# Pooled attention and grouped experts: keys and values in five blocks of 32 rows a pair, and another order for batches 0 to 2

## The chip, the cores and the metric

The kernel runs on one core of one Trainium2 chip. The metric is the device time of one execution in microseconds (us). PE (TensorE) does the matmuls, DVE (VectorE) and POOL (GpSimd) element-wise work, ACT (ScalarE) copies, casts and activations. SP (SyncE) issues most DMAs; ACT issues some. A DMA "lane" below is one of eight semaphores that the framework hands round: an issue waits until the DMA that last used its lane has landed.

## The reference

For 8 batches of 8 heads with 576 rows of 64, keys and values are averaged over groups of 8 rows (72 pooled rows a head), and attention runs over them. Its 4608 tokens of 512 numbers then go to a mixture of 16 experts (4 groups of 4), one expert a token.

```python
k_p = k.reshape(B, H, Sp, pool, D).mean(axis=3); v_p = ...      # pool = 8, Sp = 72
scores = scale * q @ k_p.T ; attn = softmax(scores)
x = (attn @ v_p).transpose(0, 2, 1, 3).reshape(B * S, H * D)
g_idx = argmax(x @ w_group) ; g_w = softmax(...)[g_idx]
e_idx = argmax(x @ w_expert[g]) ; e_w = softmax(...)[e_idx]
out[token] = g_w * e_w * (relu(x @ w1[g, e]) @ w2[g, e])        # 512 -> 1024 -> 512
```

## The kernel before

**Stages.** One batch at a time. A batch has a main expert, the one that most of its tokens choose; its tokens all go through that expert's weights, and the result is scaled by a gate that is zero for tokens of other experts. Those are done at the end, in a part called Left.

The order of the work is written out by hand, in four strings: START (batch 0's attention), FIRST (batch 0's experts beside batch 1's attention), STEADY (batches 1 to 6) and LAST. A piece such as `a.kr:0:f` is a method of a class with its arguments. The letter says whose: a is this batch's attention, m its experts, n the next batch's attention, w the next batch's weights, x the batch after that, t set-up work, l the part Left. PE, SP, DVE and POOL follow the strings in order; ACT does so in START and FIRST, and a scheduler of the framework orders it elsewhere.

**Attention (class Att).** The rows of two heads are a pair: 144 pooled rows of 512 numbers (8 rows of 64). `load_k` brings the first 128 of them for two pairs in one DMA of 128 partitions; `load_v` the same rows of v, as four blocks of 32 rows on the 32 partitions of each pair, in four DMAs; `load_r` the last 16 rows of k or v of each pair into a tile `rem`. `kr` sums the eight rows of k by three additions in place on DVE (`fold`: 256, 128, 64 wide), `vr` those of v on POOL, `rr` sums `rem` by a reduction on DVE, `vm` (POOL) splits the block that both heads share. `kb` (ACT) copies the sums into two masked halves, one for each head, `kt` transposes them on PE and copies the result to `kT`. `qt` (batch 0, by matmuls with the identity) or `qb` (DVE, other batches) transposes a chunk of 128 rows of q, `sc` makes its scores on PE, `mx`, `sb`, `su_`, `nm` are the softmax (DVE; the exponent on ACT; the last product on POOL), `pt` turns the result on DVE. `av` multiplies with the values on PE and casts the result to fp32r on ACT, `avd` gives the remainder on DVE: tokens `xt` as two parts. `rt`, `route`, `count`, `gates`, `keep_x` route the tokens. `guess_x` and `guess_e` guess the main expert ahead of time from the sums of v for batches 0 and 1; later batches count (`main_expert`). Either ends in a register that SP loads and that the weights' DMAs wait for.

**Experts (class Moe).** `load` brings a quarter of the first (1) or second (2) weights, 0.52 MB. `split` casts it to fp32r on ACT and takes the remainder on POOL. `up:f:h` is 12 matmuls for rows f of the first product and half h of the tokens (256 or 320), with an ACT evacuation; `upd` its remainder on DVE; `down:z` 8 matmuls of the second product.

`t.warm:n` are n matmuls of ones with nothing to compute. Tiles for k, `kv`, rotate over two buffers; v has one (`vv`).

Line 198 is `load_r`, 190 `load_v`, 184 `load_k`, 211 `load_q`, 251 to 253 `fold`, 246 `kb`, 266 `kt`, 283 `qt`, 431 `guess_x`, 438 `guess_e`, 494 `load`, 501 and 502 `split`, 516 `up`, 542 and 553 `down`, 348 `av`, 357 `avd`, 312 and 314 `sb`, 321 `su_`.

Of the kernel before, what the change touches and what calls it, by code (L numbers as in the profile page):

```python
# [8 lines left out]
F32 = mybir.dt.float32  # L9
F32R = mybir.dt.float32r  # L10
# [3 lines left out]
ALU = mybir.AluOpType  # L14
# [4 lines left out]
SP = 72  # L19
# [22 lines left out]
a.mx:4 a.sb:4 m.up:3:0 m.split:1:3:p m.load:2:1 m.load:2:2 m.load:2:3 n.load_qb:0 n.load_qb:1 n.load_qb:2 n.load_qb:3 m.upd:3:0 a.pt:3 a.su_:4 a.nm:4:p m.up:4:0 m.upd:4:0
m.up:5:0 m.upd:5:0 a.pt:4 m.up:6:0 m.upd:6:0 a.av:256:320 m.up:7:0 m.upd:7:0 a.avd:256:320 m.split:2:0:p
a.rt:0:256 m.up:0:1 m.upd:0:1 n.vr:0:p a.rt:256:320 m.up:1:1 m.upd:1:1 n.rr m.split:2:1:p n.vr:1:p n.vm m.up:2:1 m.upd:2:1 a.route n.kr:0:f
m.up:3:1 m.upd:3:1 n.guess_x m.split:2:2:p m.up:4:1 m.upd:4:1 a.count n.guess_e m.up:5:1 m.upd:5:1 n.kr:1:f n.kb a.gates m.split:2:3:p
# [9 lines left out]
m.load:2:3 m.up:1:1 m.upd:1:1 n.sc:2 n.mx:2 n.sb:2 n.qb:3 n.pt:1 x.load_r:k x.load_k:0 x.load_k:1 x.load_r:v x.load_v  # L55
# [5 lines left out]
m.down:0 n.rt:256:320 x.kr:0:f m.down:1 x.kr:1:f m.down:2 n.route m.down:3 m.down:4 n.main_expert w.load:1:0 w.load:1:1 w.load:1:2 w.load:1:3  # L61
x.rr x.kb m.down:5 x.qb:0 n.gates n.keep_x m.down:6 x.vr:0 x.vr:1 m.down:7 w.split:1:0 w.load:2:0 x.kt m.down:8 m.down:9
# [813 lines left out]
```

## Time and profile before

| what | value |
|---|---|
| median of 3 runs | 586.15 us (583.66 to 586.68) |
| profiled execution: time, span | 585.75 us, 584.0 us |
| busy: PE | 524.3 us (90%) |
| busy: DVE, POOL, ACT | 349.6, 242.6, 216.7 us |
| 0 to 40.4 us | START: up to the first matmul of `up` |
| 40.4 to 145.7 us | FIRST |
| 145.7 to 516.2 us | six times STEADY, 61.8 to 62.1 us each but the last (61.0) |
| 516.2 to 584.0 us | LAST and Left |

The profiled execution took 585.75 us, of which 584.0 are the span that the trace covers. Busy times are those of one engine and overlap with the others'.

### The profile page before, as it was taken

The page shows a single profiled execution, that of the slowest core. Times are in us where ns is not written, and L with a number is a line of the kernel's source. Part 1 is how long each engine was busy: PE and PEld are TensorE (multiplying, and loading weights), DVE is VectorE, ACT ScalarE, POOL GpSimd, SP SyncE. Part 2 cuts the span into 40 slices and gives each one's busy share as a digit, 9 for nine tenths or more (in the row PEclk, how much of TensorE's full clock was granted, in tenths as well). Part 3 has the DMA queues.
Part 4 walks back from the last instruction along what each step waited for, and adds up shares of the span by engine and source line. Part 5 has one row for each costly group of instructions (what it writes and reads, how often), then busy time and mean ns, then how long its engine had stood idle before and what let it go on. Part 6 is the DMA issues. An engine that isn't in the chain of part 4 may idle for free.

```text
span 584.0 us, 15213 instructions
## 1 busy us (share of the span) xinstructions
PE 524.3 (90%) x6125; PEld 460.0 (79%) x6125; DVE 349.6 (60%) x1031; ACT 216.7 (37%) x428; POOL 242.6 (42%) x201
## 2 busy tenths in 40 slices
PE   6777868696899999899989998999999998999995
PEld 6665757475797899789978897889878997899864
DVE  3367586559866567456955495738665673358702
ACT  1233431134443354334532554244433543244211
POOL 3254630353482347424660558053814572231300
PEclk9799988889999999999999999999999999999999
DMA  8196602870493639455762758095927210563731
GB/s 219 29 260 206 71 0 71 246 128 20 143 210 64 210 109 219 63 177 157 177 107 91 236 148 140 21 371 153 200 56 223 94 38 2 182 187 122 250 122 48
DMA packets 113521, 81.33 MB, mean 139 GB/s; under 512 B 70538, under 2 KB 89994, under 8 KB 113064
## 3 DMA queue, kind: packets, MB, share of 16 engines
q1 hardware_dynamic: 107872, 70.54, 47.0%
q10 hardware_dynamic: 5544, 9.74, 4.8%
q8 instruction: 50, 0.82, 0.6%
q14 instruction: 23, 0.19, 0.1%
q0 software_dynamic: 32, 0.04, 0.0%
HBM read 75.01 MB, written 28.38 MB: 177 GB/s over the span
## 4 chain that ended last, share of the span: by engine, by line
PE 70%; DVE 16%; DMA 6%; ACT 3%; issue 2%; SPq 1%; POOL 1%; ACTq 0%; DVEq 0%; POOLq 0%
PE mm L516 30%; PE mm L542 21%; PE sc L298 4%; PE mm L553 4%; PE sc L348 4%; PE tp L365 2%; DMA kv<-in_k_dram 2%; DMA out_dram<-y 2%; DVE xt L357 1%; DMA rem<-in_k_dram 1%; SPq L220 1%; DVE p L312 1%; ACT xt L353 1%; DMA rem<-in_v_dram 1%; DVE su L321 1%
## 5 line engine op out<-in xcount | busy, mean ns | idle before, releaser
L502 POOL TENSOR_TENSOR w<-sw,w 128x1024 fp32r<-128x1024 f32 x61 | 144.9, 2383 | 163.3 <-ACT w L501 163.3
L516 PE MATMUL mm<-xt,w 128*128 128x256 f32 (+1 forms) x1536 | 206.4, 292 | 4.0 <-POOL w L502 2.0
L516 PEld LDWEIGHTS mm<-xt,w 128*128 128x128 f32 x1536 | 196.0, 192 | 11.7 <-issue 3.4
L542 PE MATMUL mm<-w,ht 128*128 128x512 f32 x768 | 178.0, 385 | 0.0
L542 PEld LDWEIGHTS mm<-w,ht 128*128 128x128 f32 x768 | 142.8, 190 | 21.6 <-issue 1.9
L327 POOL TENSOR_TENSOR p<-p,su 128x576 f32<-128x576 f32 (+1 forms) x40 | 42.1, 1054 | 119.7 <-DVE su L322 88.1
L518 ACT ACTIVATE ht<-mm 128x256 fp32r<-128x256 f32 (+1 forms) x128 | 52.1, 410 | 96.3 <-PE mm L516 96.0
L501 ACT CAST w<-sw 128x1024 fp32r<-128x1024 f32 x64 | 65.9, 1043 | 25.2 <-DMA sw<-in_moe_w_dram 25.2
L528 DVE SCALAR_TENSOR_TENSOR ht<-mm,ht 128x160 fp32r<-128x160 f32 (+2 forms) x192 | 38.9, 258 | 30.4 <-ACT ht L518 29.6
L314 ACT ACTIVATE p<-p 128x576 f32<-128x576 f32 (+1 forms) x40 | 25.5, 637 | 75.6 <-DVE p L312 65.7
L308 DVE TENSOR_REDUCE mx<-sc 128x8 f32<-128x576 f32 (+1 forms) x40 | 27.6, 690 | 35.8 <-PE sc L298 35.8
L348 PE MATMUL sc<-pT,v 32*64 32x256 f32 (+1 forms) x384 | 29.8, 443 | 16.6 <-DVE xt L357 9.7
L298 PE MATMUL sc<-kT,qT 64*32 64x72 f32 x2304 | 32.5, 232 | 9.4 <-DVE qT L290 5.1
L298 PEld LDWEIGHTS sc<-kT,qT 64*32 64x32 f32 x2304 | 25.6, 106 | 17.6 <-issue 11.7
L524 DVE SCALAR_TENSOR_TENSOR ht<-mm,ht 128x256 fp32r<-128x256 f32 x64 | 26.0, 408 | 22.0 <-ACT ht L518 21.4
L547 ACT ACTIVATE y<-mm,gm 128x512 f32<-128x512 f32 x32 | 21.9, 684 | 42.9 <-PE mm L542 42.9
L348 PEld LDWEIGHTS sc<-pT,v 32*64 32x64 f32 x384 | 14.9, 142 | 23.1 <-issue 19.7
L320 DVE TENSOR_REDUCE su<-p 128x8 f32<-128x576 f32 (+1 forms) x40 | 27.1, 678 | 7.9 <-ACT p L314 7.7
L334 DVE STREAM_TRANSPOSE pT<-p 128x640 f32<-128x640 f32 (+1 forms) x40 | 30.3, 757 | 2.6 <-POOL p L327 2.6
L348 PE MATMUL tp<-pT,v 32*64 32x256 f32 (+1 forms) x384 | 31.5, 443 | 0.0
L553 PE MATMUL mm<-w,ht 128*128 128x512 f32 x128 | 29.5, 381 | 0.0
L312 DVE TENSOR_TENSOR p<-sc,mx 128x576 f32<-128x576 f32 (+1 forms) x40 | 27.9, 696 | 1.4
(196 smaller groups left out, 487.9 us busy)
## 6 DMA issues: line engine op xcount, KB each, us to landing
sw<-in_moe_w_dram SPq DMA_DIRECT2D x72, 512.0 KB
xscr<-xt SPq DMA_DIRECT2D x8, 2304.0 KB
vv<-in_v_dram SPq DMA_DIRECT2D x32, 256.0 KB
out_dram<-y ACTq DMA_DIRECT2D x32, 256.0 KB
q<-in_q_dram SPq DMA_DIRECT2D x112, 72.0 KB
kv<-in_k_dram SPq DMA_DIRECT2D x14, 512.0 KB
pT<-xscr SPq DMA_DIRECT2D x4, 1152.0 KB
kv<-in_moe_w_dram SPq DMA_DIRECT2D x4, 512.0 KB
```

The lines of the kernel that those rows point to most:

```text
L298: nc.tensor.matmul(ps[32 * g:32 * g + 32, x, SP * t:SP * t + SP], lhsT=s.qT[c][64 * x:64 * x + 64, g, 32 * t:32 * t + 32], rhs=s.kT[64 * x ...
L312: tt(out=p.rearrange("p t (x s) -> p x t s", x=2), in0=s.ss[c][:, :, 0:SP * w].rearrange("p x (t s) -> p x t s", s=SP), in1=bc(s.m[c][:, : ...
L327: (nc.vector if eng == "v" else nc.gpsimd).tensor_tensor(out=p, in0=p, in1=bc(s.su[c][:, 0:w], SP), op=ALU.mult)
L334: nc.vector.transpose(out=s.pT[:, :, o:o + n].rearrange("p j (t i) -> p t j i", i=32), in_=probs[(s.b * NC + c) % 2][:, 0:n // 32].rearran ...
L348: nc.tensor.matmul(banks[a][64 * x:64 * x + 64, 0:n], lhsT=s.v6[32 * a:32 * a + 32, 5 if x and i == 0 else j, :], rhs=s.pT[32 * a:32 * a + ...
L501: nc.scalar.copy(out=wh, in_=raw)
L502: (nc.vector if eng == "v" else nc.gpsimd).tensor_tensor(out=wl, in0=raw, in1=wh.bitcast(F32), op=ALU.subtract)
L516: nc.tensor.matmul(ps[:, 0:n], lhsT=l[:, kc, fs], rhs=apart(xt[:, r, kc, sl]), start=(kc == 0 and i == 0), stop=(kc == 3 and i == 2))
L518: nc.scalar.activation(out=halves(ht[:, sl]), in_=joined(ps[:, 0:n]), func=AF.Relu)
L528: stt(out=ht[:, at:at + hi - lo], in0=ps[:, a, lo:hi], scalar=0.0, in1=ht[:, t + lo:t + hi].bitcast(F32), op0=ALU.max, op1=ALU.subtract)
L542: nc.tensor.matmul(ps, lhsT=s.ht[f][:, 640 * l + o:640 * l + o + 128], rhs=apart(s.w[2, f // 2][r][:, f % 2, :]), start=(i == 0), stop=(i ...
L553: nc.tensor.matmul(ps, lhsT=s.ht[f][:, 512:640], rhs=apart(s.w[2, f // 2][r][:, f % 2, :]), start=(i == 0), stop=(i == 15))
```

## The change

Keys and values of a pair of heads are now five blocks of 32 pooled rows (160 rows, of which the last 16 are the first ones of the next pair and are masked or left unread). `load_kv` brings them in one DMA a pair, 32 partitions of 5 x 2 KB, for k and v alike: eight DMAs a batch, 2.62 MB, in place of fourteen. `load_r`, `rr`, `kb` and the masks `sel` go. `kr` has a part of two blocks and a part of three, and its last addition writes both halves by a broadcast; `kt` makes five transposes of which none is special. `kv` and `vv` have one buffer each; batch 0's k lies in a buffer of `pT`.

For batch 0, `guess_r` sums raw v over rows and heads by 40 matmuls, `vsum` makes the pooled values by 8 matmuls with the identity; POOL pools nothing there. q comes as two DMAs of 256 rows (pieces of 512 bytes) and `sc` of chunks 1 and 2 writes to the banks of the experts' products. `split` can be called as `cast` (ACT) and `lo` (the remainder).

START, FIRST and a new string SECOND (batch 1) have another order; `qt` and `sc` of chunk 3 move from START to FIRST; the second half of batch 1's values, its routing and batch 2's first pooling move from FIRST to SECOND. 32 matmuls of ones replace 48. STEADY changes only in the names of the pooling. The strings' rows follow as PE, POOL and SP get them; of the strings the diff shows a line each.

```diff
 START = """
-t.load_wr a.load_r:k:a a.load_r:v:a a.load_k:0:h a.load_k:1:h a.load_v a.load_q:0 a.load_q:1 a.load_q:4
+t.load_wr a.load_k:p a.load_q:0 a.load_v a.load_q:1 a.load_q:4
...
 STEADY = """
-m.load:2:3 m.up:1:1 m.upd:1:1 n.sc:2 n.mx:2 n.sb:2 n.qb:3 n.pt:1 x.load_r:k x.load_k:0 x.load_k:1 x.load_r:v x.load_v
+m.load:2:3 m.up:1:1 m.upd:1:1 n.sc:2 n.mx:2 n.sb:2 n.qb:3 n.pt:1 x.load_k x.load_v
...
-    sk = ctx.enter_context(tc.tile_pool(name="sk", bufs=2))
+    sk = ctx.enter_context(tc.tile_pool(name="sk", bufs=1))
...
+        def load_kv(s, t, x, eng="s"):
+
+            d = nc.scalar if eng == "a" else nc.sync
+            x = x.rearrange("b h (s j) d -> (b h s) (j d)", j=8)
+            for a in range(4):
+                o, p = H * SP * s.b + 2 * SP * a, t[32 * a:32 * a + 32]
+                y = x[o:o + 128].rearrange("(j i) x -> i j x", i=32)
+                if o + 160 <= B * H * SP:
+                    d.dma_start(out=p, in_=x[o:o + 160].rearrange("(j i) x -> i j x", i=32))
...
+        def kr(s, u, eng="f"):
+            if u == 0:
+                s.kbt = wk.tile([128, NC, 2, D], F32, name="kb")
+            z = slice(0, 2) if u == 0 else slice(2, 5)
+            e = nc.vector if eng == "f" else nc.gpsimd
+            a = s.fold(s.k[:, z], e)
+            e.tensor_tensor(out=s.kbt[:, z], in0=a[:, :, 0:64].unsqueeze(2).broadcast_to([128, z.stop - z.start, 2, D]),
+                            in1=a[:, :, 64:128].unsqueeze(2).broadcast_to([128, z.stop - z.start, 2, D]), op=ALU.add)
...
-        def rr(s):
-            red(out=s.vtile()[:, 4, :], in_=s.rem.rearrange("p (j d) -> p d j", j=8), axis=AX.X, op=ALU.add)
...
+        def vsum(s):
+
+            ps = ps_t.tile([128, 512], F32, name="tp")
+            for j in range(8):
+                nc.tensor.matmul(ps[:, 0:NC * D], lhsT=ident, rhs=s.v[:, :, D * j:D * j + D], start=(j == 0), stop=(j == 7))
+            v6 = s.vtile()
+            nc.scalar.copy(out=v6[:, 0:NC], in_=ps[:, 0:NC * D].rearrange("p (j d) -> p j d", d=D))
...
+        def guess_r(s):
+
+            ps = ps_t.tile([128, 512], F32, name="tp")
+            for t in range(NC):
+                for j in range(8):
+                    nc.tensor.matmul(ps[0:64, 0:8], lhsT=s.v[:, t, D * j:D * j + D], rhs=heads[:, :, t, :], start=(t == 0 and j == 0), stop=(t == 4 and j == 7))
...
-            run(FIRST if b == 0 else LAST if b == B - 1 else STEADY, b)
+            run(FIRST if b == 0 else SECOND if b == 1 else LAST if b == B - 1 else STEADY, b)
```

PE in START, before (mm<-ones are the matmuls of ones, tp<-ident,ht the router weights, tp<-ident,q a chunk of `qt`, sc<-kT,qT a chunk of scores, tp<-heads,v the guess from pooled values and tp<-wr,gx its second half):

```order
L824 MATMUL mm<-ones 128x128 x22
L813 MATMUL tp<-ident,ht 128x20 x4
L824 MATMUL mm<-ones 128x128 x8
L266 MATMUL tp<-ident,kb 128x128 x4
L270 MATMUL tp<-ident,krz 128x128
L824 MATMUL mm<-ones 128x128 x2
L283 MATMUL tp<-ident,q 64x128 x8
L824 MATMUL mm<-ones 128x128 x2
L298 MATMUL sc<-kT,qT 32x72 x32
L283 MATMUL tp<-ident,q 64x128 x8
L431 MATMUL tp<-heads,v_220 64x4 x10
L824 MATMUL mm<-ones 128x128 x2
```

And now (tp<-heads,vv is the guess on raw v, tp<-vv,ident the value sums):

```order
L832 MATMUL tp<-ident,ht 128x20 x4
L843 MATMUL mm<-ones 128x128 x4
L279 MATMUL tp<-ident,q 64x128 x8
L843 MATMUL mm<-ones 128x128 x2
L263 MATMUL tp<-ident,kb 128x128 x5
L300 MATMUL sc<-kT,qT 32x72 x32
L279 MATMUL tp<-ident,q 64x128 x8
L300 MATMUL mm<-kT,qT 32x72 x32
L444 MATMUL tp<-heads,vv 64x8 x40
L279 MATMUL tp<-ident,q 64x128 x8
L452 MATMUL tp<-wr,gx 128x20 x4
L254 MATMUL tp<-vv,ident 128x320 x8
```

The scores of two chunks now stand ahead of the guess, and the value sums behind it; the transposes of k have lost their remainder.

PE in FIRST around batch 1's guess and keys, before (mm<-xt,w are products of `up`, tp<-ident,lt is `route`, tp<-oh,ones the count, tp<-ident,kb the keys):

```order
L373 MATMUL tp<-ident,lt 128x40 x4
L373 MATMUL tp<-ident,lt 64x40
L516 MATMUL mm<-xt,w 128x320 x12
L431 MATMUL tp<-heads,v_874 64x4 x10
L516 MATMUL mm<-xt,w 128x320 x12
L406 MATMUL tp<-oh,ones 128x80
L438 MATMUL tp<-wr,gx 128x20 x4
L516 MATMUL mm<-xt,w 128x320 x12
L266 MATMUL tp<-ident,kb 128x128 x4
L270 MATMUL tp<-ident,krz 128x128
```

And now:

```order
L377 MATMUL tp<-ident,lt 128x40 x4
L377 MATMUL tp<-ident,lt 64x40
L535 MATMUL mm<-xt,w 128x320 x12
L410 MATMUL tp<-oh,ones 128x80
L535 MATMUL mm<-xt,w 128x320 x12
L263 MATMUL tp<-ident,kb 128x128 x5
L435 MATMUL tp<-heads,v_770 64x4 x10
L535 MATMUL mm<-xt,w 128x320 x12
L452 MATMUL tp<-wr,gx 128x20 x4
L535 MATMUL mm<-xt,w 128x320 x24
```

The count stands nearer to `route`, the guess behind the keys, and each of them with products between.

SP in FIRST where batch 1's first weights and batch 2's keys and values are loaded, before (lf is `keep_x`'s register, xscr<-xt its store):

```order
L494 DMA sw<-in_moe_w_dram 128x4x256
L494 ISA
L494 DMA sw<-in_moe_w_dram 128x4x256
L184 DMA kv<-in_k_dram 128x2x512 x2
L198 DMA rem<-in_k_dram 16x512 x4
L198 DMA rem<-in_v_dram 16x512 x4
L190 DMA vv<-in_v_dram 32x4x512 x4
L220 DMA q<-in_q_dram 32x18x32 x16
```

And now:

```order
L508 DMA sw<-in_moe_w_dram 128x4x256
L508 ISA
L508 DMA sw<-in_moe_w_dram 128x4x256
L182 DMA vv<-in_v_dram 32x5x512 x4
L182 DMA kv<-in_k_dram 32x5x512 x4
L508 ISA
L508 DMA sw<-in_moe_w_dram 128x2x512
L508 ISA
L508 DMA sw<-in_moe_w_dram 128x2x512
L219 DMA q<-in_q_dram 32x18x32 x16
```

Fourteen copies have become eight; v goes first, and two pieces of weights stand ahead of q.

## Rows read from the trace of the kernel before

**Rows 1.** The page's part 4: the chain that ended last, shares by engine.

```profile
PE 70%; DVE 16%; DMA 6%; ACT 3%; issue 2%; SPq 1%; POOL 1%; ACTq 0%; DVEq 0%; POOLq 0%
```

**Rows 2.** Windows by stage: length; PE, PEld, DVE, ACT, POOL busy (instructions); clock, DMA share, GB/s.

```profile
40.40:94.20 53.80, 39.87 (x400) 35.01 (x399) 35.64 (x88) 17.38 (x38) 23.32 (x17) 0.87 0.43 92
94.20:145.70 51.50, 41.42 (x605) 32.52 (x604) 34.47 (x76) 15.96 (x31) 18.69 (x16) 0.93 0.52 132
145.70:207.80 62.10, 57.50 (x640) 50.75 (x639) 40.20 (x129) 25.05 (x51) 29.76 (x22) 1.00 0.63 162
207.80:269.70 61.90, 60.10 (x719) 53.17 (x718) 38.83 (x116) 26.07 (x51) 29.34 (x22) 1.00 0.58 146
```

**Rows 3.** PE's waits from 40 to 146 us: total, times, longest (us).

```profile
PE tp L266 <- ACT kb L246: 7.0, 2, 4.6
PE sc L348 <- DVE p L312: 5.5, 1, 5.5
PE tp L431 <- POOL v L261: 3.0, 1, 3.0
...
PE mm L516 <- POOL w L502: 2.0, 1, 2.0
PE tp L406 <- DVE oh L400: 1.9, 1, 1.9
```

**Rows 4.** Windows of 1 us in START, columns as in rows 2.

```profile
4.00:5.00 1.00, 1.00 (x9) 1.00 (x8) 0.69 (x4) 0.00 (x0) 0.28 (x3) 1.00 1.07 377
...
7.00:8.00 1.00, 1.00 (x11) 0.88 (x9) 0.93 (x3) 0.00 (x0) 0.00 (x0) 1.00 1.07 174
...
14.00:15.00 1.00, 0.85 (x4) 0.33 (x4) 0.00 (x0) 0.46 (x2) 0.89 (x2) 0.87 1.08 309
15.00:16.00 1.00, 0.04 (x1) 0.00 (x0) 0.00 (x0) 0.00 (x0) 1.00 (x2) 0.50 1.02 247
```

**Rows 5.** Timeline of START: start, length (us), engine, line, operation, [idle before].

```profile
4.80 0.69 DVE L251 TENSOR_TENSOR ht<-ht 128x512 f32<-128x512 f32 x1 [0.28 <-DMA ht<-in_k_dram]
...
12.69 1.26 POOL L251 TENSOR_TENSOR vv<-vv 128x512 f32<-128x512 f32 x1 [8.31 <-DMA vv<-in_v_dram]
...
22.78 1.09 PE L283 MATMUL tp<-ident,q 128*64 128x128 f32 x16
...
23.70 0.70 PE L431 MATMUL tp<-heads,v 128*64 128x4 f32 x20
...
29.21 2.11 SPq L494 DMA_DIRECT2D sw<-in_moe_w_dram  x4
...
32.64 1.05 ACT L501 CAST w<-sw 128x1024 fp32r<-128x1024 f32 x1 [0.86 <-DMA sw<-in_moe_w_dram]
...
34.26 2.35 POOL L502 TENSOR_TENSOR w<-sw,w 128x1024 fp32r<-128x1024 f32 x1
...
38.23 0.76 DVE L357 TENSOR_TENSOR xt<-sc,xt 128x256 fp32r<-128x256 f32 x2 [0.40 <-ACT xt L353]
...
40.40 2.92 PE L516 MATMUL mm<-xt,w 128*128 128x256 f32 x24
```

**Rows 6.** Timeline of FIRST, columns as in rows 5.

```profile
46.52 2.25 DVE L321 TENSOR_SCALAR su<-su 128x8 f32<-128x8 f32 x1
...
111.33 0.68 ACT L314 ACTIVATE p<-p 128x576 f32<-128x576 f32 x1 [9.89 <-DMA kv<-in_k_dram]
```

**Rows 7.** Windows of 5 us in FIRST, columns as in rows 2.

```profile
85.00:90.00 5.00, 3.39 (x13) 2.99 (x12) 3.67 (x9) 1.16 (x4) 2.43 (x1) 0.50 0.00 0
...
115.00:120.00 5.00, 5.00 (x54) 3.31 (x52) 3.46 (x9) 1.64 (x5) 3.00 (x2) 0.50 1.14 217
```

**Rows 8.** Timeline of a steady stage, columns as in rows 5.

```profile
218.62 1.79 SPq L198 DMA_DIRECT2D rem<-in_k_dram  x4
...
229.68 9.46 SPq L220 DMA_DIRECT2D q<-in_q_dram  x16
...
242.66 0.68 DVE L251 TENSOR_TENSOR kv<-kv 128x512 f32<-128x512 f32 x1
```

More of the change, by code (lines that the diff above doesn't have):

```diff
@@ L42 @@
[L42 to L45, printed above, removed]
@@ L186, in load_v @@
-        def load_v(s, eng="s"):
-            t = s.v = sk.tile([128, 4, 512], F32, name="vv", bufs=1)
-            x = s.rows(v)[0:128].rearrange("(j i) g x -> g i j x", i=32)
-            for a in range(4):
-                (nc.scalar if eng == "a" else nc.sync).dma_start(out=t[32 * a:32 * a + 32], in_=x[a])
-        def load_r(s, which, eng="s"):
-            if s.rem is None:
-                s.rem = sk.tile([128, 512], F32, name="rem", bufs=1)
-            o, f = (16, k) if which == "k" else (0, v)
-            for a in range(4):
-                (nc.scalar if eng == "a" else nc.sync).dma_start(out=s.rem[32 * a + o:32 * a + o + 16, :], in_=s.rows(f)[128:144, a, :])
+            s.xt = s.lt = s.v6 = s.pT = s.q = s.k = s.v = None
@@ L290, in qb, with sc @@
             nc.vector.transpose(out=s.qT[c][:, :, 0:n], in_=s.q[:, 0:NG * S].rearrange("p (g t) -> p g t", g=NG)[:, :, o:o + n])
-        def sc(s, c):
-            ps = s.ss[c] = ps_s.tile([128, 2, 512], F32, name="sc")
+        def sc(s, c, where="s"):
+            if where == "s":
+                ps = ps_s.tile([128, 2, 512], F32, name="sc")
+                s.ss[c] = [(slice(0, 2), ps)]
+                ps = [ps[:, 0], ps[:, 1]]
+            else:
+                ps = [ps_m.tile([128, 512], F32, name="mm") for i in range(2)]
+                s.ss[c] = [(slice(x, x + 1), ps[x].unsqueeze(1)) for x in range(2)]
             w = CH[c][1] // 32
@@ L433, in guess_x @@
             nc.scalar.copy(out=s.gx, in_=ps[:, 0:4])
+        def guess_r(s):
[3 more added lines that the diff above has]
+                    nc.tensor.matmul(ps[0:64, 0:8], lhsT=s.v[:, t, D * j:D * j + D], rhs=heads[:, :, t, :], start=(t == 0 and j == 0), stop=(t == 4 and j == 7))
+            s.gx = sm.tile([128, NG], F32, name="gx", bufs=1)
+            for x in range(2):
+                nc.scalar.copy(out=s.gx[64 * x:64 * x + 64], in_=ps[0:64, 4 * x:4 * x + 4])
         def guess_e(s):
@@ L495, in load, with cast, lo @@
             s.raw[m, j] = raw
-        def split(s, m, j, eng="p"):
-            raw = s.raw[m, j]
-            wh = wp.tile(list(raw.shape), F32R, name="w")
-            wl = wp.tile(list(raw.shape), F32R, name="w")
-            nc.scalar.copy(out=wh, in_=raw)
-            (nc.vector if eng == "v" else nc.gpsimd).tensor_tensor(out=wl, in0=raw, in1=wh.bitcast(F32), op=ALU.subtract)
-            s.w[m, j] = (wh, wl)
+        def cast(s, m, j):
+            raw = s.raw[m, j]
+            s.w[m, j] = (wp.tile(list(raw.shape), F32R, name="w"), wp.tile(list(raw.shape), F32R, name="w"))
+            nc.scalar.copy(out=s.w[m, j][0], in_=raw)
+        def lo(s, m, j, eng="p"):
+            wh, wl = s.w[m, j]
+            (nc.vector if eng == "v" else nc.gpsimd).tensor_tensor(out=wl, in0=s.raw[m, j], in1=wh.bitcast(F32), op=ALU.subtract)
+        def split(s, m, j, eng="p"):
+            s.cast(m, j)
+            s.lo(m, j, eng)
         def up(s, f, hf):
```

147 lines of the change are left out of this document (71 added, 76 removed).

## Prediction

> **What bounds the kernel now.** I read the chain that ended last first: seven tenths of it are PE, the next shares are DVE and DMA [rows 1]. So time is gained where PE stands still, and the table of stages says where that is [rows 2]. In a steady stage (the last row, batch 2's) PE is busy for 60.10 of 61.90 us at the full clock: 1.8 us to be had, whatever is done to pooling. [...] Third, PE's waits in the two middle stages [rows 3]: they name single events (batch 1's keys for the transposes, its softmax, its values, a weight), not a repeated cost. The change rewrites these stages and leaves the order of the steady ones, so nearly all of the sum lies before 207.8 us.
>
> **Start (term A).** The first guess of an expert waits for v. Before, its matmuls start at 23.70, the expert's weights are issued at 29.21, the first piece's cast starts at 32.64, its remainder is ready at 34.26 + 2.35, and the first product starts at 40.40 because the attention in front of it ends late (its last evacuations on DVE begin at 38.23) [rows 5]. Now, by steps:
> - Transfers. k and v both go in copies of 32 partitions. Rows of before: the 128-partition copies of k moved 377 GB/s, the 32-partition copies of v 174 and q's pieces of 1 KB 309 [rows 4]. I take 200 for k and v, 250 for q's pieces of 512 bytes (bounds for these: 309, and 1.18 MB in the 9.46 us over which q's 16 copies in pieces of 128 bytes are issued, 125 GB/s [rows 8]). k is 1.31 MB, so 6.6 us after a first byte at about 2.7: 9.4. The first half of q, 0.52 MB, 2.1 us: 11.6. v, 6.5 us: 18.1.
> - k is folded on DVE in 2560 elements of additions at 0.69 us for 512 [rows 5]: 3.5 us, done near 13.2; transposes, copy and the scores of chunks 0 and 1 (I take for each the 1.09 of a chunk of q's transposes [rows 5]) fill PE to about 18, beside the wait for v.
> - The guess on raw v is 80 records where the old one had 20 in 0.70 us [rows 5]: 2.9 us at that rate, 5.8 at half the clock. I take 2.9: PE works just before it. It takes the place of the POOL folds (1.26, then shorter ones, per half, which stood behind v for 8.31 us [rows 5]). End: 21.0.
> - From the end of the old guess matmuls (24.4) to the weight issue passed 4.8 us. Same instructions after it, so issue at 25.8; the weight lands 3.4 us later as before: 29.2; cast 1.05, remainder 2.35: 32.6. The value sums (16 records on PE, hidden at any price up to these 3.4 us) and the softmax of chunks 0 and 1 lie beside this wait. The last evacuations now stand behind that cast and end near 34.0. First product from 33.0, not 40.40: **-7.4**.
>
> [...] In the rows, k at 128 partitions moved 377 GB/s and pieces of 32 about half [rows 4]. [...] In the rows' terms the loss is 1.31/0.20 less 1.05/0.377, 3.8 us for k, and it is already in the 9.4.
>
> **Batch 0's experts and batch 1 (terms B, C, D).** B, what goes: the wait of batch 1's guess for pooled v, 3.0 (POOL gets v's folds ahead of the weights' remainders); the two waits of the transposes for kb, 7.0 together (kb was written on ACT after DVE; DVE's last addition now writes it, and more products stand ahead of the transposes); a weight remainder, 2.0 [rows 3]. And 5.5 for softmax (L348 on DVE p): the exponent on ACT started at 111.33 after 9.89 us that the trace puts on the landing of k [rows 6], since ACT had to issue a store of y whose DMA lane was last used by the loads of batch 2. The order below has them earlier, and six fewer copies in a batch. Sum: **-17.5**. [...] I count 3.5 + 3.0 = **-6.5** of the 8.1. D, what comes: q transposes and scores of chunk 3 moved out of the start, 2.0 (1.09 [rows 5] and somewhat less for the scores); a stretch at half the clock where PE has little to do between 29.5 and 32.6, 2.0; the count's matmul, which comes one product after route's transposes where it came three after, 2.6 (the nearest row: batch 1's count waited 1.9 for the end of that chain on DVE [rows 3]; bounds 0 and twice that); and 3.0 for DVE instructions held up by POOL (one took 2.25 us on 8 elements a partition while POOL ran a remainder [rows 6]; five such pieces stand in these stages). **+9.6**. In all B + C + D = -14.4, so the stretch of 167.4 becomes 153.0. What is queued behind the moved instructions: on PE's queue the products; on ACT the casts, behind which the up-evacuations wait; on SP the copies of batch 2, which now alternate with weights.
>
> Batch 1's second half of values, its routing and batch 2's keys move behind batch 1's first product. That is PE work which I neither add nor subtract: it lies inside 40.4 to 207.8 before and after.
>
> **Steady stages.** Per batch POOL's folds of 5 blocks cost, for the larger part of three blocks, between 1.26 (512 elements) and 2.35 (1024 [rows 5]), POOL being busy less than half of 61.90 [rows 2]. On DVE 2560 elements of additions take the place of 1792 and of a reduction, which differ by less than 1 us at 0.69 for 512; ACT loses its copies for kb; PE has the same five transposes. All zero, as PE never waits there. The copies take 2.62 MB at 200, 13.1 us, where k (1.05 MB at 377), v (1.05 at 200) and the remainders (0.26 at 200) took 2.8 + 5.2 + 1.3 = 9.3: +3.8 us, hidden, since they go out from 218.62, q behind them by 229.68, and k is first read at 242.66 [rows 8]: some 10 us of room. The last stage is left at zero.
>
> **Sum.** -7.4 - 14.4 = -21.8 against the profiled run's 585.75 (span 584.0): 564.0; the median of the runs is 0.4 above that run: **564**.
>
> **Rivals.**
> 1. No wait of its own in the new order (D only 2.0 of 9.6): 7.6 less, **556**. For it: nothing forces the waits, and steady stages in such an order have 1.8 us. [...] Against: in steady stages the pooling is a whole batch ahead. Chance 0.16.
> 2. Transfers hold the start. At the low row of 174 GB/s k and v need 7.5 each, and q's piece at 125 GB/s 4.2: v lands 3.9 later. With the guess at half the clock (+2.9) the start gains 0.6 only: **571**. For it: the clock was at half from 15 us on in the start [rows 4], after a wait. Against: the new start has PE work in that time. Chance 0.12.
> 3. DVE holds the middle stages. It is busy 35.64 + 34.47 + 40.20 = 110.3 of 167.4 us there, 66%, against 63% in a steady stage [rows 2]; the forecast needs 72%. If 66% is what an in-order DVE between POOL's locks can do, the stretch stays at 167 and only A is left: **579**. For it: three of PE's waits end on DVE or behind it, and many DVE instructions hang on a POOL result. Chance 0.13. [...]
> 4. The other side: the copies come too late in steady stages. k, v and q's 1.18 MB (9.46 us) go out from 218.62 [rows 8] and are needed by about 250: 22 us for 2.62 MB, 119 GB/s. Below that each of five batches waits; from 97 GB/s (27 us, 5 us late, 25 in all) it eats the whole gain, and the time is **590**. For it: k and v have one buffer now, so a late fold holds the next load too. Against: the row of 32-partition copies has 174 [rows 4]. Chance 0.06.
>
> **Chances and range.** The forecast has 0.53. A measurement of this kernel tells about 0.5% (2.9 us) from no change. Cases 1 to 3 and the forecast are all faster, but a quarter of case 3 spreads above 583: 0.04 no change; with 0.01 of the small end of case 4, same 0.05. Slower 0.05, faster 0.90. The range leaves out the 548 end, the top of case 3 and case 4: **552 to 580**.
>
> **What would show it.** In the trace of after: v landing near 18, the first weights issued near 26, the first product near 33 (A); no PE wait over 3 us on POOL v, on kb or on softmax p between 33 and 186, and a clock of 0.95 or more in that stretch (B, C); batch 2's first product near 186 against 207.8; steady stages of 61.9 within 0.3. I am wrong in A if k or v lands over 3 us later; in D if PE's waits on DVE in batch 0's experts exceed 10 us; in the steady term if their period moves by 0.5 us or more.

## The result, and the profile after

The changed kernel takes 591.43 us (589.24 to 593.21, 6 runs) against 586.23 (583.66 to 587.01, 6 runs) beside it: a ratio of 1.0095, 95% interval 1.0066 to 1.0124. It is slower by about 1%, where 564 was forecast. The profiled execution has a span of 589.0 us against 584.0. Executions of one kernel differ by some us (before: 582.58 to 590.62 over all its runs here), and the first product of the kernels below that have the new START with the raw guess lies at 43.42 to 46.13 where nothing ahead of it was changed; so a place in a trace is good to about 2 us, and times of kernels are compared by medians. Ratios leave out an execution over 1.5% above its kernel's fastest, medians do not.

The windows of after, cut by work: first product of batch 0, first down product, first product of batch 1, of batch 2, of batch 3:

```profile
44.31:92.90 48.59, 39.17 (x413) 35.53 (x413) 31.16 (x87) 18.55 (x40) 26.64 (x19) 0.89 0.63 128
92.90:130.77 37.87, 32.93 (x458) 26.55 (x457) 24.94 (x49) 11.75 (x20) 10.79 (x7) 0.95 0.77 197
130.77:213.53 82.76, 71.19 (x850) 60.51 (x849) 55.65 (x163) 27.17 (x56) 29.92 (x24) 0.94 0.46 109
213.53:275.45 61.92, 60.12 (x717) 53.20 (x716) 39.09 (x115) 27.02 (x50) 37.38 (x28) 1.00 0.68 164
```

[Rows 2] has its third cut at 145.70, where FIRST ends; batch 1's first product came 8 us before that. Before, cut by the same work, up to batch 2's first product:

```profile
40.40:94.06 53.66, 39.73 (x400) 34.87 (x399) 35.64 (x88) 17.38 (x38) 23.32 (x17) 0.87 0.43 92
94.06:137.55 43.49, 35.65 (x452) 27.65 (x451) 27.25 (x62) 12.59 (x26) 16.33 (x15) 0.92 0.61 154
137.55:207.64 70.09, 63.25 (x792) 55.59 (x790) 47.42 (x143) 28.43 (x56) 31.97 (x23) 1.00 0.56 145
```

The first product comes at 44.31 and not at 40.40 [rows 5]; from there to batch 2's first product pass 169.2 us where 167.2 passed; the rest takes 375.5 where it took 376.4. The steady row is that of before to 0.02 us. By stage, after is 5.1 and 5.6 us shorter up to batch 1's first product, and 12.7 longer from there, where work was moved to. In the middle PE is busy for 143.3 us, so it stands still for 25.9 (28.6 before), and slow clock costs, by an estimate from the windows (busy time times what the granted clock lacks of 1.00), 39.17 x 0.11 + 32.93 x 0.05 + 71.19 x 0.06 = 10.2 (8.1 before): 36.1 us where 36.7 stood before. The figures of before are from [rows 2]: 39.87 + 41.42 + 57.50 = 138.8 us busy of 167.4 leave 28.6, and 39.87 x 0.13 + 41.42 x 0.07 = 8.1.

The start of after, columns as in [rows 5]:

```profile
9.79 0.69 DVE L231 TENSOR_TENSOR pT<-pT 128x512 f32<-128x512 f32 x1 [5.26 <-DMA pT<-in_k_dram]
...
17.38 0.80 PE L300 MATMUL mm<-kT,qT 64*32 64x72 f32 x54 [0.69 <-ACT qT L281]
21.95 0.47 PE L300 MATMUL mm<-kT,qT 64*32 64x72 f32 x10 [3.76 <-issue]
22.35 8.59 PE L444 MATMUL tp<-heads,vv 128*64 128x8 f32 x79
...
34.51 6.32 PE L254 MATMUL tp<-vv,ident 128*128 128x320 f32 x16
...
37.01 2.78 SPq L508 DMA_DIRECT2D sw<-in_moe_w_dram  x4
...
41.71 1.04 ACT L514 CAST w<-sw 128x1024 fp32r<-128x1024 f32 x1
```

k is there at 9.8, as forecast. But PE stops in the middle of the scores of chunk 1, 54 records in, and goes on 3.76 us later with the last 10, "issue", waiting for no engine and no data that the trace names. Then the guess runs for 8.6 us, the value sums for 6.3, and the weights go out at 37.01, not 25.8. The clock in windows of 1 us (columns as in [rows 2]):

```profile
18.00:19.00 1.00, 0.18 (x18) 0.01 (x1) 0.00 (x0) 0.04 (x1) 0.00 (x0) 1.00 1.22 281
20.00:21.00 1.00, 0.00 (x0) 0.00 (x0) 0.00 (x0) 0.00 (x0) 0.00 (x0) 1.00 0.02 1
22.00:23.00 1.00, 1.00 (x16) 0.80 (x17) 0.52 (x2) 0.00 (x0) 0.00 (x0) 0.50 0.00 0
36.00:37.00 1.00, 1.00 (x3) 0.61 (x3) 0.95 (x3) 0.00 (x0) 0.00 (x0) 0.50 0.00 0
```

PE is busy in every microsecond from 22 to 37 and runs at half the clock all the time (1.00 busy and 0.50 granted in each). Its waits from 44 to 214 us, columns as in [rows 3]:

```profile
PE tp L410 <- DVE oh L404: 10.0, 3, 6.1
PE sc L352 <- DVE pT L338: 5.3, 2, 4.3
PE sc L300 <- DVE qT L286: 3.0, 1, 3.0
PE sc L300 <- DVE cr L486: 2.4, 1, 2.4
...
PE mm L535 <- POOL w L518: 0.5, 1, 0.5
PE tp L263 <- DVE kb L227: 0.4, 1, 0.4
```

The waits of [rows 3] for kb, for pooled v and for a weight are gone or under 0.6: 11.1 of their 12.0 us. The softmax of a late chunk is still waited for (5.3 in all). The count on the routing, which waited 2.0 over the same stretch of before, waits 10.0 in three places, and 2.4 on `cr` (a product of `keep_x`) and 2.0 of "issue" are new. The wait for q's transposes is not new; before had

```profile
PE sc L298 <- DVE qT L290: 5.1, 3, 2.8
```

### The profile page after: what moved, and what is told of

The parts are those of the page before. It is cut to its first block, busy times and chain, and to the rows that moved or that the text cites. A ratio compares the mean times of both kernels' runs of the same rounds, so it can differ in the third digit from the quotient of the medians.

```text
span 589.0 us, 15210 instructions
## 1 busy us (share of the span) xinstructions
PE 538.2 (91%) x6169; PEld 472.4 (80%) x6169; DVE 347.9 (59%) x1024; ACT 211.4 (36%) x406; POOL 243.0 (41%) x193
## 5 line engine op out<-in xcount | busy, mean ns | idle before, releaser
L535 PE MATMUL mm<-xt,w 128*128 128x256 f32 (+1 forms) x1536 | 209.1, 295 | 3.5 <-ACT xt L357 1.2
L535 PEld LDWEIGHTS mm<-xt,w 128*128 128x128 f32 x1536 | 198.8, 194 | 11.2 <-issue 3.3
L561 PE MATMUL mm<-w,ht 128*128 128x512 f32 x768 | 180.3, 388 | 0.0
L311 DVE TENSOR_REDUCE mx<-sc 128x8 f32<-128x576 f32 (+1 forms) x38 | 26.0, 684 | 37.2 <-PE sc L300 37.2
L352 PE MATMUL sc<-pT,v 32*64 32x256 f32 (+1 forms) x384 | 28.1, 422 | 13.4 <-DVE xt L361 8.1
L300 PE MATMUL sc<-kT,qT 64*32 64x72 f32 x2176 | 31.2, 230 | 9.6 <-DVE qT L286 3.0
L300 PEld LDWEIGHTS sc<-kT,qT 64*32 64x32 f32 x2176 | 24.2, 105 | 17.8 <-issue 14.4
L352 PE MATMUL tp<-pT,v 32*64 32x256 f32 (+1 forms) x384 | 29.6, 423 | 0.0
L572 PE MATMUL mm<-w,ht 128*128 128x512 f32 x128 | 29.3, 381 | 0.0
L316 DVE TENSOR_TENSOR p<-sc,mx 128x576 f32<-128x576 f32 (+1 forms) x38 | 26.4, 694 | 1.4
```

Source lines behind the costliest of these rows:

```text
L300: nc.tensor.matmul(ps[x][32 * g:32 * g + 32, SP * t:SP * t + SP], lhsT=s.qT[c][64 * x:64 * x + 64, g, 32 * t:32 * t + 32], rhs=s.kT[64 * x ...
L352: nc.tensor.matmul(banks[a][64 * x:64 * x + 64, 0:n], lhsT=s.v6[32 * a:32 * a + 32, 5 if x and i == 0 else j, :], rhs=s.pT[32 * a:32 * a + ...
L535: nc.tensor.matmul(ps[:, 0:n], lhsT=l[:, kc, fs], rhs=apart(xt[:, r, kc, sl]), start=(kc == 0 and i == 0), stop=(kc == 3 and i == 2))
L561: nc.tensor.matmul(ps, lhsT=s.ht[f][:, 640 * l + o:640 * l + o + 128], rhs=apart(s.w[2, f // 2][r][:, f % 2, :]), start=(i == 0), stop=(i ...
L572: nc.tensor.matmul(ps, lhsT=s.ht[f][:, 512:640], rhs=apart(s.w[2, f // 2][r][:, f % 2, :]), start=(i == 0), stop=(i == 15))
```

## The experiments

Each kernel is compared with before on its own chip (586.4 to 586.9 there). "First product" and so on are places in its trace.

**Which part loses.** Three kernels split the change: the five blocks alone, with the orders of before; the new START alone; the new FIRST and SECOND alone.

```diff
 e1_blocks: START, FIRST of before, names of the pooling changed
-run(FIRST if b == 0 else SECOND if b == 1 else ...
+run(FIRST if b == 0 else LAST if b == B - 1 else STEADY, b)
 e2_start: START of after; FIRST of before, with
+ ... a.nm:2:p a.qt:3 a.sc:3 m.upd:0:0 ...
 e3_order: START of before; FIRST (without a.qt:3, a.sc:3) and SECOND of after
```

> Five blocks and one buffer for k and v alone, with the orders of before (START, FIRST, and STEADY for batch 1). Theory S (the loss is made in the new START, by the guess on raw v): within 2 us of before, 584 to 588, first product of batch 0 near 40, steady stages 61.9. Theory O (the loss is made by the new order of FIRST and SECOND): the same. Rival L (the 32-partition copies and single buffers cost in themselves): 590 or more, with v landing after 18 us and waits for k or v in FIRST.

> The new START with the FIRST and STEADY of before (q transposes and scores of chunk 3 at the head of FIRST). Theory S: the first product stays near 44 and nothing behind it makes up for the 3.9 us and the 2.0 us of work moved behind it: 590 to 593. Theory O: the start's delay is taken up by slack in FIRST: 585 to 588.

> The START of before (on five blocks) with the new FIRST and SECOND. From the first product to batch 2's first product the trace of after has 169.2 us against 167.2 of before, 2.0 of it work moved in. Theory S: the new order is worth about nothing, first product near 40, time 584 to 588. Theory O: the order itself loses 4 to 6 us in SECOND: 590 to 593.

Measured: the blocks alone 586.39, ratio 0.9987 (0.9960 to 1.0013), no difference. The new START alone 598.16, 1.0121 (1.0035 to 1.0206). The new order alone 580.98, 0.9898 (0.9882 to 0.9915). So the copies and single buffers cost nothing that shows, the loss is made with START, and the order is worth some 5 us, not the 14.4 of the forecast. Theory S holds for where the loss is, but two of its three ranges were missed: the second run's median (of 4 runs, 589.99 to 598.92) lies above its 590 to 593 and the third below its 584 to 588. START costs 11.8 us by the medians of e2 and e1 and 10.4 by those of after and e3, of which the first product's delay is about 5; the rest is lost behind it (in e2 the products of batch 0 took 64.1 us at a mean clock of 0.79).

**What in START.** First the guess through POOL as before, in the new START:

```diff
-... a.mx:1 a.guess_r a.sb:1 ... a.vsum n.load_v ...
+... a.mx:1 a.vr:0 a.vr:1 a.vm a.guess_x a.sb:1 ... n.load_v ...
```

> The changed kernel, but batch 0's values are pooled on POOL and guessed from the sums as before; no guess on raw v and no value sums on PE. Theory S in its narrow form (the price of the raw guess, 8.6 us, and what runs at half the clock with it): POOL needs about 6.5 us from v's landing near 17, so the guess ends near 25 and not 31, the first product comes at 38 to 40, and the time is 585 to 587. Rival (what costs is the 4 us in which PE stands still before the guess and the half clock after it, whoever guesses): first product still at 43 or later, 590 to 592.

584.62, ratio 0.9982 (0.9945 to 1.0019). Its trace has the same gap (3.68 us of "issue"), POOL folds v from 17.99 to 24.85, the weights go out at 31.67, the first product comes at 38.29: 6 us earlier than in after. The narrow theory holds (its range, 585 to 587, was missed by 0.4). But the pooled guess does not bring back all that START lost: with a first product 1.2 us earlier than the order alone has it, the kernel is 3.6 us slower. Nor does it end the half clock, which stands here without any raw guess:

```profile
26.00:27.00 1.00, 1.00 (x14) 1.00 (x12) 0.00 (x0) 0.51 (x1) 0.20 (x1) 0.50 0.00 0
44.00:45.00 1.00, 1.00 (x11) 0.67 (x7) 0.72 (x1) 0.00 (x0) 0.00 (x0) 0.50 1.06 203
```

So what the raw guess costs in the chain to the first product is shown, and the half clock behind it is not its work alone. Next, matmuls of ones between the gap and the guess:

```diff
-... a.mx:1 a.guess_r ...
+... a.mx:1 t.warm:14 a.guess_r ...
```

> The changed kernel with 14 matmuls of ones between the scores of chunk 1 and the guess on raw v. In after PE stood still for 3.8 us before the guess, and the granted clock was 0.50 from 21 to 38 us while PE was busy all that time; the guess took 8.6 us (107 ns a record), the value sums 6.3. Theory W (the raw guess does not bring the clock back, wide matmuls do): clock 1.00 by 26 us, the guess at about 54 ns a record, 4.3 us, all behind it at the full clock, weights issued 1 to 3 us earlier than 37.0, time 587 to 590. Rival P (the clock falls to half again during the guess, or the record's price does not hang on the clock): weights issued at 38 to 40, 592 to 594.

595.39 (590.03 to 599.61, 4 runs), 1.0120 (1.0032 to 1.0207); the weights are issued at 40.24, 3 us later than in after. Time and issue lie above rival P's ranges. Its windows:

```profile
26.00:27.00 1.00, 1.00 (x7) 1.00 (x7) 0.00 (x0) 0.00 (x0) 0.24 (x1) 0.50 0.00 0
28.00:29.00 1.00, 1.00 (x21) 1.00 (x19) 0.00 (x0) 0.00 (x0) 0.00 (x0) 1.00 0.00 0
30.00:31.00 1.00, 1.00 (x17) 1.00 (x16) 0.00 (x0) 0.00 (x0) 0.00 (x0) 0.76 0.00 0
31.00:32.00 1.00, 1.00 (x11) 1.00 (x11) 0.00 (x0) 0.00 (x0) 0.00 (x0) 0.50 0.00 0
```

The clock comes back behind 5 us of the ones, which start at 22.14 (granted 0.95 in the microsecond from 27, 1.00 in that from 28), the guess starts at 27.81, and 3 us later the clock is at half again (0.50 in the microsecond from 31) though PE is shown as busy all the time. Rival P's first half is right: a guess begun at the full clock does not keep it. Theory W's price is right too: 6.4 us at a mixed clock, where 80 records at the 107 ns of after would take 8.6. An estimate from these, with t us at the full clock and half of 107 a record there (the windows show 21 records at 1.00 and 11 at 0.50): t/0.0535 + (6.4 - t)/0.107 = 80 gives t = 2.2, near the 3 us seen. Third, the late half of q, to see what the gap is:

```diff
-a.load_v a.load_q:1 a.load_q:4
+a.load_v
-... a.sb:0 a.sc:1:m ...
+... a.sb:0 a.load_q:1:a a.load_q:4:a a.sc:1:m ...
```

> The changed kernel with the second half of q and its last rows issued on ACT behind the exponent of chunk 0, so that their 0.66 MB start about 15 us later on. Theory F (PE's next instructions wait behind the copies in the DMA queues; in after it went on 2.7 us after they ran dry at 19.2): the gap in the scores of chunk 1 ends 1.5 to 3 us earlier than 21.95, the guess starts near 19.5, time 587 to 590. Rival N (the gap has another cause, say the bank or the values of v): the guess starts at 21.5 to 22.5 as before, time 590 to 593.

587.16, 1.0009 (0.9976 to 1.0042). Its timeline:

```profile
17.89 0.80 PE L302 MATMUL mm<-kT,qT 64*32 64x72 f32 x54 [0.68 <-ACT qT L283]
19.26 0.34 PE L302 MATMUL mm<-kT,qT 64*32 64x72 f32 x10 [0.57 <-issue]
19.54 7.09 PE L446 MATMUL tp<-heads,vv 128*64 128x8 f32 x79
```

The gap stands behind the same 54 records (the order up to them is the same, so the record by itself tells little) but lasts 0.57 us, and PE goes on at 19.26 for 21.95: with these copies held back, what it waits for comes 2.7 us earlier. The trace has a packet that fits, in a queue of the kind "instruction". After has one of them in the window from 19.2 to 20.7 us, and nothing else but small packets (packets, MB, share of 16 engines):

```profile
q8 instruction: 1, 0.02, 5.7%
```

It holds 16,384 bytes, begins at 19.24, when the copies run dry (DMA share 1.22 in the microsecond from 18, 0.28 in that from 19), and ends at 20.62; PE goes on at 21.95. Here it lies at 16.63 to 17.92, and PE goes on at 19.26. In all eleven kernels with the new START, PE goes on 1.2 to 1.4 us after its end. That it carries PE's own instructions is inferred from this timing, since the packet names no engine.

The guess starts at the full clock and loses it within 2.5 us (granted 1.00 in the microsecond from 20, 0.50 in that from 22), as in the run before. In after the clock had fallen in the gap, before the guess (0.52 in the microsecond from 21). Theory F holds; first product 40.61. Both together:

```diff
+a.load_q:1:a a.load_q:4:a behind a.sb:0; a.vr:0 a.vr:1 a.vm a.guess_x for a.guess_r, no a.vsum
```

> Two undone parts together: the second half of q late on ACT (which ended the gap) and batch 0's values pooled and guessed through POOL (no raw guess, no value sums on PE). Theory S+F (gap and raw guess make the start's loss, and add up): POOL ends its folds near 24 or earlier, first product at 35 to 38 against 44.3, time 578 to 582. Rival (POOL's pooling is late by itself or the clock stays at half without PE work): first product 38.5 or later, 583 to 586.

584.85, 0.9979 (0.9932 to 1.0026), first product 37.89. The first product lies in the theory's range, the time in the rival's (583 to 586). The two gains don't add up: PE waits 3.8 us for POOL's sums in place of the gap, which is 1.27 here.

**The waits in the middle.** Four edits of after, each at one wait:

```diff
 e7_nm4:    -n.nm:4:p  +n.nm:4:v                     (FIRST's end)
 e8_count:  -n.kr:1 a.count m.up:4:1 ... n.guess_x a.gates
            +n.kr:1 m.up:4:1 ... n.guess_x a.count a.gates
 e9_lock:   -m.up:3:1 m.cast:2:2 m.lo:2:2 ... m.up:4:1
            +m.up:3:1 ... m.up:4:1 m.cast:2:2 m.lo:2:2
 e10_load:  -w.load:1:3 x.load_v ... x.load_k ... w.load:2:0 w.load:2:1
            +w.load:1:3 ... w.load:2:0 x.load_v w.load:2:1 x.load_k
```

> The changed kernel with the last softmax product of batch 1 on DVE instead of POOL, where it stands behind two weights' remainders and a fold of v. Theory Q (PE's 4.3 us wait for the turned chunk 4 of batch 1 at 135 us is made by that queue, and the slow clock behind it too): the wait is under 1 us, batch 1 reaches its first down product 4 to 6 us earlier, time 585 to 588. Rival H (the time comes back as another wait within 20 us): the wait is gone, time 590 to 592.

589.89, 1.0037 (1.0010 to 1.0063). The wait is 3.2 in place of 4.3, neither theory: on DVE the product takes 2.35 us (133.22 to 135.57), and POOL runs two remainders from 130.56 to 135.24 beside it. Another wait for the same tile, at 117.8, grew from 1.1 to 2.4. The kernel is some 0.6% faster than after, whose interval lies above this one.

> The changed kernel with the count of batch 0 two products later, behind the keys' transposes and the guess of batch 1. In after its matmul waited 6.1 us for the routing on DVE, and PE ran at half the clock for some 7 us behind it. Theory R (this wait and its clock cost about 8 us): no PE wait over 2 us there, clock above 0.9 from 75 to 92, first down product of batch 0 at 86 to 88 instead of 92.9, time 584 to 587. Rival D (DVE is what is full there; the transposes wait for the keys' sums on DVE instead): a wait of 3 us or more on kb, gain under 3 us, 588 to 592.

592.81, 1.0111 (1.0069 to 1.0152), 0.8 above rival D's range. The edit put the count behind one piece of `up`, the keys' transposes and the guess, not two products later, and rival D's move came: the wait went to the transposes of the keys.

```profile
PE tp L263 <- DVE kb L227: 6.8, 1, 6.8
```

> The changed kernel with one cast and remainder of batch 0's second weights moved behind the count, so that POOL runs it after the routing on DVE. In after one of the 15 short instructions of the routing took 2.31 us in place of about 0.18 while POOL ran that remainder, and the count on PE waited 6.1 us. Theory K (DVE is held for the length of the remainder): no routing instruction over 0.6 us, the count's wait 4.0 us or less, first down product 1 to 4 us earlier with the clock behind it, 587 to 590. Rival (the routing is late for other reasons, the folds of the keys ahead of it): wait still over 5.5 us, 590 to 593.

589.19, 1.0044 (1.0019 to 1.0069). No routing instruction takes over 0.32 us and the count waits 4.0: theory K, by just the length that DVE was held (2.31 - 0.18 = 2.1 us, and 6.1 - 4.0 = 2.1). Here is the held one in after (2.31 us), and the same in this run:

```profile
77.19 2.31 DVE L393 TENSOR_TENSOR og<-rg,m 128x20 f32<-128x20 f32 x1
```

```profile
77.62 0.18 DVE L393 TENSOR_TENSOR og<-rg,m 128x20 f32<-128x20 f32 x1
```

> The changed kernel with the copies of batch 2's v and k each behind one more piece of batch 1's weights. In after ACT stood 8.1 us before the exponent of batch 1's first chunk, because the store of y ahead of it waited for a copy of v to land, while DMA was full from 96 to 112 us. Theory Y (the store's lane is held by that burst of copies): ACT's wait on DMA under 3 us, no PE wait over 1.5 us between 95 and 115, batch 1's first product 2 to 5 us earlier than 130.8, 586 to 590. Rival M (the wait goes to a later store, or to v and k for batch 2): ACT waits for another landing between 110 and 130, 590 to 593.

591.74, 1.0092 (1.0053 to 1.0131). ACT's wait of 8.1 us for a landing and q's 3.0 on PE are gone, batch 1's first product comes at 128.26 against 130.77, and then the turned chunk 4 is waited for 8.3 us: rival M in effect, though it isn't another landing. The same edit on the order without the new START:

> The START of before with the new FIRST and SECOND, as in the run that took 581, and the later copies of batch 2's v and k. Theory Y: 2 to 5 us better than 581, 576 to 579. Rival M: 580 to 583.

583.50, 0.9959 (0.9937 to 0.9980), and there the wait for chunk 4 is 12.5 us: neither theory, and the time is 2.5 us above that of the run without the edit. Last the keys' folds on POOL, as a test of DVE:

```diff
-n.kr:0 ... n.kr:1      (FIRST)
+n.kr:0:p ... n.kr:1:p
```

> The changed kernel with batch 1's folds of the keys in FIRST on POOL instead of DVE (some 4 us of DVE instructions with their hold-ups). Theory D (DVE is what is full between 70 and 92 us, so the count waits): the count's wait falls from 6.1 to 4 us or less, batch 0's first down product comes 2 to 5 us earlier after the first product than the 48.6 of after, time 586 to 589. Rival (POOL's folds then hold DVE, or the keys come late from POOL): the wait on the count or on kb stays at 5 us or more, 590 to 593.

591.08, 1.0082 (1.0056 to 1.0108); the count waits 7.0. The rival, by its own mechanism: with POOL's folds beside it, the routing on DVE is held up.

```profile
75.97 1.78 DVE L387 TENSOR_TENSOR de<-el,m 128x20 f32<-128x20 f32 x1
77.78 1.73 DVE L389 SCALAR_TENSOR_TENSOR re<-de,desc 128x20 f32<-128x20 f32 x1
77.67 1.80 POOL L231 TENSOR_TENSOR kv<-kv 128x768 f32<-128x768 f32 x1
```

In after the two DVE instructions take 0.18 each, and the routing's chain 5.75 us where it takes 8.15 here. DVE's busy time up to the first down product fell by 2.2 us only (28.92 for 31.16). So the run took work off DVE and put waits in its place; whether DVE's own work makes the count wait it does not tell.

**Where the order's gain goes.** The new order up to batch 0's last product of `up`, then the down part and STEADY of before:

```diff
 START of before
 FIRST: lines of after up to m.up:7:1 m.upd:7:1 (without a.qt:3, a.sc:3)
+n.qb:0 n.sc:0 n.mx:0 n.sb:0 n.qb:1 w.load:1:2 w.load:1:3
+m.down:0 n.su_:0 n.nm:0:p x.load_k x.load_v m.down:1 ...   (as before)
 batch 1: STEADY
```

> The START of before, the products of FIRST in the new order, the down part of FIRST in the order of before, and STEADY for batch 1 (nothing put off to a SECOND). From the traces: the new order of the products takes 43.4 us where the old one takes 54.8; the old down part 40.1 and 69.6 for batch 1, against 39.1 and 84.9 with the new down part and SECOND. Theory G (the gain of the products is given back in the down part and SECOND): batch 2's first product at 192 to 198 us against 206.8, time 571 to 577. Rival (the old down part only works because of what its products had left behind; waits of the same size come in their place): batch 2's first product at 201 or later, time 579 to 584.

575.30 (570.92 to 576.05), ratio 0.9785 (0.9724 to 0.9846): faster than both kernels, by 1.5 to 2.8% against before. Its windows, cut as above, and those of the blocks alone:

```profile
39.63:91.20 51.57, 37.98 (x399) 34.45 (x397) 30.78 (x91) 16.37 (x35) 24.04 (x17) 0.90 0.53 109
91.20:128.91 37.71, 34.98 (x457) 27.29 (x451) 28.09 (x56) 12.54 (x23) 17.36 (x15) 0.95 0.78 182
128.91:198.54 69.63, 63.24 (x791) 55.59 (x790) 46.97 (x143) 27.21 (x53) 31.28 (x22) 1.00 0.61 148
```

```profile
39.47:94.31 54.84, 39.55 (x399) 35.77 (x398) 36.57 (x87) 16.47 (x35) 24.33 (x17) 0.88 0.48 98
94.31:134.41 40.10, 35.17 (x453) 26.96 (x451) 25.56 (x60) 12.21 (x23) 16.71 (x15) 0.96 0.73 175
134.41:204.03 69.62, 63.23 (x791) 55.60 (x790) 47.12 (x143) 27.20 (x53) 31.20 (x22) 1.00 0.59 148
```

Batch 1's stage is the same 69.6 at the full clock; in after it takes 82.76 at 0.94. Batch 2's first product comes at 198.54, just past the 192 to 198 of theory G, and 5.5 us ahead of the blocks alone. Batch 0's products take 51.57 us here where 43.4 was expected: PE waits 2.5 us for scores of batch 1's first chunk, which here stand ahead of the first down product, and 3.2 on ACT for tokens, a wait that the next run doesn't have. The median moved by more, 11 us against the blocks' 586.39, whose profiled execution, 581.19, was the lowest of its ten. With the keys on POOL as well:

> As the run before, with batch 1's folds of the keys on POOL in the products of FIRST. Theory D: 1 to 4 us under the run before. Rival: the same time or longer.

576.30 (574.65 to 579.90), 0.9847 (0.9791 to 0.9903): the same within the noise, as the rival says. POOL's folds stand beside the routing here too.

## Why the prediction was wrong, point by point

The span was forecast at 564.0 - 1.75, about 562, and is 589. Of the 27 us, 11.3 are A (44.31 against 33.0: 4.3 that the guess starts later, 5.8 that it runs longer, 1.2 behind it), 16.2 the middle (169.2 against 153.0), and -0.9 the rest.

**A, the step "the guess on raw v is 80 records ... 2.9 us at that rate".** It failed, and with it "I take 2.9: PE works just before it". A record took 107 ns at half the clock (8.59 us over 80), and at the full clock, by an estimate from the windows of e5, about half of that (21 records in a microsecond at 1.00, 11 at 0.50); the row I scaled from had 35 ns. I had called half the clock the upper bound, 5.8: the price and the clock both went to their worse end. In after the premise failed already ahead of the guess, for PE stood still and the clock was at 0.52 when the guess began; but the two runs that began it at the full clock with PE at work just before (e5, e6) lost it within 2 to 3 us, so the premise would not have kept the clock. Shown busy time does not tell it here: in e5 PE is shown as busy for the whole of each microsecond from 28 to 31, and the granted clock goes from 1.00 to 0.76 in that from 30 and 0.50 in that from 31. What takes the clock away no run shows.

**A, the step "scores of chunks 0 and 1 fill PE to about 18".** PE did, to 18.2, and then stood for 3.76 us; the guess began at 22.35, not 18.1. v was not the reason: POOL folds it from 17.99 in the run with the pooled guess, so the transfers came as forecast. Of rival 2, then, the late v did not come, but its other half, the guess at half the clock, did. Holding back 0.66 MB of q took the gap to 0.57 at the same record. The instruction packet of 16,384 bytes begins when the copies run dry, and PE goes on 1.2 to 1.4 us after it ends, whether that is at 20.62 (on at 21.95) or, with the copies held back, at 17.92 (on at 19.26). That PE waits for instructions, and that they wait behind the copies, is inferred from this timing and shown no further, as the packet names no engine. The forecast had no term for it.

The rest of A: from the guess's end to the weights 6.0 us, not 4.8, at half the clock; then 4.7 to the cast, not 3.4. The value sums were called hidden at any price up to 3.4 us. They took 6.3, and the cast at 41.71 stands directly behind ACT's copies of them:

```profile
40.87 0.43 ACT L256 COPY v<-tp 128x320 f32<-128x320 f32 x1 [7.33 <-PE tp L254]
41.19 0.52 ACT L258 ACTIVATE v<-tp,share 128x64 f32<-128x64 f32 x2
```

Still, little of it shows: e4, which has no value sums, casts 4.7 us after the issue as well, and its first product comes 6.6 us after the issue where after's comes 7.3.

**B.** Of the waits for v, kb and the weight, 12.0 us, 11.1 went, as forecast. The 5.5 did not: "the order below has them earlier" failed. ACT again stood 8.1 us for a landing, now of v, and q's 3.0 and slow clock came of it. At that time the store of the tokens, four pieces of weights and the copies are under way together (341 to 359 GB/s at 96 to 102 us); holding v and k back by a piece of weights ends ACT's wait (e10). The fewer copies of the new load did not end it; what share each transfer has in it no run tells.

**C.** No gain: slow clock costs 10.2 us there where it cost 8.1 and 1.6 was forecast. No run shows the 3.5 + 3.0 of this term. What the traces show is the granted 0.50 in two stretches of 5 us of before, with PE busy for 3.39 and 5.00 of them [rows 7], and in after the waits at 76, 110, 133, 152 and 200 us, each followed by a stretch at 0.50 (in windows of 1 us, from 80, 114, 138, 155 and 202), and the one on `cr` at 160, which is not (1.00 from 160 to 164).

**D.** 9.6 were forecast for what comes: 2.0 of moved work and 7.6 of waits and clock. Standing still and slow clock were 36.7 before (the 548 of the range is what about 4 in their place, A's 7.4 and 2.0 of moved work come to); less the 11.1 that went they would be 25.6, and they are 36.1, so 10.5 came where 7.6 were forecast, and C's 6.5 did not go. By this count the 16.2 of the middle are 5.5 of B, 6.5 of C, 2.9 of D, and some 1.3 of smaller ends (0.9 of B, and moved work). "The count's matmul ... 2.6" was 6.1 in batch 0, and 10.0 for the three counts of the middle. The term had the right place and, as one term, the wrong kind of price: e7 to e10 show that a wait here is the end of a chain through DVE, POOL and ACT, and moving the one that PE shows uncovers the next (6.1 on the count became 6.8 on the keys; 3.0 on q became 8.3 on chunk 4). Rival 3, that DVE holds the stages, is not refuted. The stretch is 169.2, near its 167, with DVE busy for 31.16 + 24.94 + 55.65 = 111.8 us of it, 66%, the very share that it named; the run with the old down part has 158.9, DVE busy for 105.8, 67%. Whether that share is a limit no run shows: e13, meant to test it, lengthened DVE's chain through POOL. The rival was right in the held instructions, its "locks": e9 gave back 2.1 us of them one for one (2.31 us became 0.18, and the count's wait of 6.1 became 4.0). Rivals and forecast were priced one at a time, and parts of two came together: rival 2's guess at half the clock and rival 3's middle.

**What I did not cost.** "That is PE work which I neither add nor subtract" was said of what moved behind batch 1's first product. The work does cancel, the waits do not: batch 1's stage took 82.76 us where it takes 69.62 with the blocks alone, 13.1 more. Of these 3.7 are work at the full clock, 5.2 standing still (11.6 for 6.4) and 4.3 slow clock (71.19 x 0.06). The run with the old down part and STEADY shows the same by medians: the new products alone gain 11.1 us against the blocks (575.30 for 586.39), and with the new down part and SECOND 5.4 are left (580.98), so these two, changed together, give back about half. Which of the waits makes the most of that stays open; of those in SECOND's stage only the first, on chunk 4, was tried (e7), for a gain of some 0.6% with 3.2 us of the wait left.

**Steady stages** came out as forecast, 61.92, and rival 4 did not come.

## What to carry to other kernels

Price a new kind of matmul by a row of its own shape, and ask what the clock does during it, not only before it: many small ones with a weight load each took 8.6 us at half the clock where 2.9 were priced, and lost the full clock within 3 us where they were begun at it. Where a rewritten order removes waits, sum what is left between two fixed points of the program (here 36.7 us before and 36.1 after) before any removed wait is counted as a gain. And split such a change by stage: here the blocks were neutral, START a loss, the down part with SECOND gave back about half of what the new order of the products had gained, and that order by itself gave 2.2% (1.5 to 2.8).

## What the runs showed of the hardware

PE stopped for 3.6 to 3.8 us inside a run of equal matmuls as the copies of the start came to their end (in after from 18.2, DMA share 1.22 in the microsecond from 18 and 0.28 in that from 19), behind the same 54 records, and for 0.57 us when 0.66 MB of them went out later (e6; 1.27 with the pooled guess besides, e11). An instruction packet of 16,384 bytes began as the copies ran dry, and PE went on 1.2 to 1.4 us after it ended, in each of eleven kernels (after: 20.62 and 21.95; e6: 17.92 and 19.26). The granted clock fell from 1.00 to 0.50 within 3 us of the start of 128x64 weight loads with 8 columns each, with PE at work before and shown busy throughout (e5, e6); a record of these took 107 ns at 0.50 (after). A DVE instruction on 20 elements a partition took 2.31 us while POOL ran a remainder of 2.34 (after), and 0.18 without it (e9). With folds on POOL in place of remainders, two of the same size took 1.78 and 1.73 us, the second beside a fold of 1.80 (e13).
